# Linear attention and a gated feed-forward layer: the first batch's k and v on 128 partitions, and another order for the kernel's head

## The chip, the cores and the metric

The kernel runs on one core of a Trainium2 chip. Its engines work side by side, each through its own list of instructions in order: TensorE (PE in the profile, with its weight loads as PEld), VectorE (DVE), ScalarE (ACT), GpSimd (POOL) and SyncE (SP). They wait for one another by semaphores. DMA transfers are issued from the lists of SP, ACT and POOL. The metric is the device time of one execution in microseconds (us), the median of the runs.

## The reference

```python
batch, n_heads, seq, head_dim = (8, 8, 576, 64)

def _attn_ref(q, k, v, g_norm):
    kv = np.einsum('bhsd,bhse->bhde', k, v)
    out = np.einsum('bhsd,bhde->bhse', q, kv)
    rms = np.sqrt(np.mean(out * out, axis=-1, keepdims=True) + 1e-06)
    return (out / rms * g_norm).astype(np.float32)

def _moe_ref(x, w_gate, w_val, w_out):      # x: (4608, 512), d_ff 1536
    gate = 1.0 / (1.0 + np.exp(-(x @ w_gate)))
    val = x @ w_val
    return (gate * val @ w_out).astype(np.float32)
```

The attention has no softmax: for each head kv = k^T v (64 x 64, summed over the 576 tokens), then q times kv, then a norm over the 64 values. The heads of one token side by side are a row of x. q, k and v are float32, the three weights float64; the result is float32.

## The kernel before

The 4608 tokens are nine chunks of 512. Chunk 0 goes through a plain first and second layer (the last 64 tokens of batch 0 belong to chunk 1). Chunks 1 to 8 go through a version of the two layers that forms sums of blocks and needs fewer products (`first_layer_fast`, `second_layer_fast`, L1017 and L1120); its matmuls, L1037 and L1139, are most of the time. The change touches what comes before all this, called the head here: the attention of batch 0, the conversion of the first weight units, and the first two blocks of chunk 0's first layer.

**Loads.** `load_kv` (L91) and `load_q` (L100) load pair n (two heads) of batch 0, for n from 0 to 3, into the pool `first` with a buffer for each pair. Token s stands on partition s // 6, so a load of k or v has 96 partitions, and on each of them, for each of the two heads, six tokens in a row: 192 pieces of 1536 bytes. The loop at L298 issues on SP, in this order: k, v, q of pair 0; of pair 1; the gate half of weight unit 0; pair 2; the value half of unit 0; pair 3. Then `w1` and `w2` issue units 1 and 2 (`load_unit`, L153). A unit is a block of 128 columns of w_gate and of w_val, 512 KB each. It is staged as raw float64 in one of three buffers (`st`), so unit 3 can load only when unit 0 has been read, and so on.

**Conversion.** `convert` (L194) makes float32 weights of a staged unit: five steps on VectorE (s0 to s4) and two on ScalarE (a0 after s0, a1 after s1; s2 waits for a0, s3 for a1, s4 for s2 and s3). In the head, the two halves of units 0, 1 and 2 are converted one by one; s4 also multiplies by g_norm. From unit 3 on, `convert_step` does a unit at a time between the later matmuls.

**Attention of a pair** (`attention`, L335): KV is k^T v, `kv_mm` at L341, six steps j of 96 tokens and in each a matmul for either head, head e writing partitions 64e to 64e+63 of one PSUM bank; KVO copies it out on VectorE; Q turns q by six transposes (L356) and QO copies it on ScalarE; U multiplies, 20 matmuls of 64 x 64 (L373); SQ (ScalarE), SUM (VectorE), ROOT (ScalarE) and NORM (VectorE, reciprocal and product) are the norm; X transposes back (L400) and XO copies x to its place on ScalarE. One PSUM tile serves all Q, another bank all KV, and two tiles take U and X in turn: Q1 waits for QO0, KV1 for KVO0, U2 for XO0.

**Blocks.** `b0` and `b1` are the first two 128-column blocks of chunk 0's first layer (`Plain`, L659). `bf.i.m` is one matmul of 512 columns (L666): half i (gate or value) of block f with pair m of x. It needs that half's s4 and XO of pair m. G and E are the sigmoid and the product behind a block. `b0` uses the two banks that the fillers and KV use before.

**Order.** The pools are under a manual schedule: each engine gets its instructions in the order in which the program emits them. For the head this is the string `order` (L699), read token by token at L708: `KV0` or `XO3` is a step of a pair, `g1.3` or `v1.3` is step s3 of unit 1's gate or value half, `ag` and `av` are the ScalarE steps, `w3` loads unit 3, and `warm10` is ten matmuls of the identity with itself (L727), whose result nobody reads. Behind the head the dense stage runs: the other ten blocks of chunk 0 (`plain`, L678), with the attention of batch 1 between them, then its second layer.

Of the kernel before, what the change touches and what calls it, by code (L numbers as in the profile page):

```python
# [10 lines left out]
FP32 = mybir.dt.float32  # L11
# [10 lines left out]
def kernel(  # L22
# [11 lines left out]
    nc = tc.nc  # L34

    B, H, S, HD = q.shape
    T, DM = out.shape
    DF = moe_w_gate.shape[1]
    P = 128
    NHP = H // 2  # L40
    NJ = 6
    NP = S // NJ
    JH = NJ // 2


    PH = P // 2
# [38 lines left out]
    first = first_ctx.__enter__()  # L85
# [3 lines left out]
    pairs = {n: {} for n in range(B * NHP)}  # L89

    def load_kv(n):  # L91
        if n >= NE:
            return
        b, h0 = n // NHP, 2 * (n % NHP)
        for name, src in (("k", k), ("v", v)):
            t = first.tile([NP, 2, NJ * HD], FP32, tag=name, name=name)
            nc.sync.dma_start(out=t, in_=src[b, h0:h0 + 2].rearrange("h (p j) d -> p h (j d)", j=NJ))
            pairs[n][name] = t

    def load_q(n):  # L100
# [52 lines left out]
    def load_unit(u, halves=(0, 1)):  # L153
        if u >= len(units):
            return
        kind, f = units[u]
        if 0 in halves:
            staged[u] = raw.tile([P, 2, DM], I64, tag="st", name="st", bufs=NST)
        st = staged[u]
        for i in halves:  # L160
            if kind == "gv":
                src = (moe_w_gate, moe_w_val)[i].rearrange("(m p) f -> p m f", p=P)[:, :, P * f:P * f + P]
                nc.sync.dma_start(out=st[:, i].rearrange("p (m f) -> p m f", m=NMT), in_=src)
            else:
                nc.sync.dma_start(out=st[:, i], in_=moe_w_out[P * (f + i):P * (f + i) + P, :])
# [143 lines left out]
    w1 = const.tile([P, N3, 4 * NMT, 2, P], FP32, name="w1")  # L309
    w2 = const.tile([P, NFT, DM], FP32, name="w2")  # L310
    ident = const.tile([P, P], FP32, name="ident")
# [23 lines left out]
    def attention(n, at_ps):  # L335

        b, m = divmod(n, NHP)
        d = {}
        kv = kvq[:, m // 2, m % 2]

        def kv_mm():  # L341
            d["kv"] = ps = at_ps("kv")
            for j in range(NJ):
                js = slice(HD * j, HD * j + HD)
                for e in range(2):
                    nc.tensor.matmul(ps[HD * e:HD * e + HD, 0, 0:HD], pairs[n]["k"][:, e, js], pairs[n]["v"][:, e, js],  # L346
                                     start=(j == 0), stop=(j == NJ - 1))

        def kv_out():
            nc.vector.tensor_copy(out=kv, in_=d["kv"][:, 0, 0:HD])  # L350

        def q_mm():
            d["q"] = ps = at_ps("q")
            for j in range(NJ):
                c0 = NP * (j % JH)
                nc.tensor.transpose(ps[:, j // JH, c0:c0 + NP], pairs[n]["q"][:, j].rearrange("p e d -> p (e d)"),  # L356
                                    ident[0:NP, 0:NP])

        def q_out():
            d["qT"] = qTs[:, S * (n % 2):S * (n % 2) + S]  # L360
            nc.scalar.copy(out=d["qT"].rearrange("p (i n) -> p i n", i=2), in_=d["q"][:, :, 0:JH * NP])  # L361

        def u_mm():


            ps = at_ps("u")
            d["u"] = ps[:, :, 0:NU * HD]
            for i in range(2 * NU):
                t0 = min(PH * i, S - PH)
                r = PH * (i % 2)  # L370
                for e in range(2):
                    es = slice(HD * e, HD * e + HD)
                    nc.tensor.matmul(d["u"][r:r + PH, e, HD * (i // 2):HD * (i // 2) + HD],  # L373
                                     d["qT"][es, t0:t0 + PH], kv[es], start=True, stop=True)

        def u_square():
            d["sq"] = sqs[:, NU * P * (n % 2):NU * P * (n % 2 + 1)].rearrange("p (e c) -> p e c", e=2)
            nc.scalar.activation(out=d["sq"], in_=d["u"], func=AF.Square)

        def u_sum():  # L380
            d["ms"] = sb.tile([P, 2, NU], FP32, tag="ms", name="ms")
            nc.vector.tensor_reduce(out=d["ms"].rearrange("p e i -> p (e i)"),
                                    in_=d["sq"].rearrange("p e (i d) -> p (e i) d", d=HD), axis=AX.X, op=ALU.add)

        def u_root():
            nc.scalar.activation(out=d["ms"], in_=d["ms"], func=AF.Sqrt, bias=eps, scale=1.0 / HD)

        def u_norm():

            nc.vector.reciprocal(d["ms"], d["ms"])  # L390
            d["xn"] = d["sq"].rearrange("p e c -> p (e c)")
            nc.vector.tensor_tensor(out=d["xn"].rearrange("p (i e d) -> p e i d", e=2, d=HD),
                                    in0=d["u"].rearrange("p e (i d) -> p e i d", d=HD),
                                    in1=d["ms"].unsqueeze(3).to_broadcast([P, 2, NU, HD]), op=ALU.mult)

        def x_mm():
            d["x"] = ps = at_ps("x")
            for i in range(NU):
                bank, c0 = divmod(P * i, UX)
                nc.tensor.transpose(ps[:, bank, c0:c0 + P], d["xn"][:, P * i:P * i + P], ident)  # L400

        def x_out():

            s0 = 0
            while s0 < S:
                c, o = divmod(S * b + s0, G)
                i, r = divmod(s0, UX)
                n_ = min(G - o, (UX if i == 0 else S - UX) - r)
                nc.scalar.copy(out=chunk(c)[:, m, o:o + n_], in_=d["x"][:, i, r:r + n_])
                s0 += n_  # L410

        return [kv_mm, kv_out, q_mm, q_out, u_mm, u_square, u_sum, u_root, u_norm, x_mm, x_out]


# [220 lines left out]
    def at_ps():  # L635
        return psum.tile([P, NAT, 512], FP32, tag="at", name="at")
# [11 lines left out]
    warm, pair_kv = bank(0), bank(1)  # L648
# [29 lines left out]
    def plain(c, u, ps, steps_at):  # L678
# [18 lines left out]


    order = """  # L699
        w1 w2 warm10 KV0 warm4 Q0 KVO0 QO0 warm3 U0 KV1 KVO1 Q1 SQ0 QO1 SUM0 ROOT0 g0.0 warm4 U1 NORM0 SQ1 warm5 X0  # L700
        SUM1 ag0.0 ROOT1 g0.1 ag0.1 NORM1 XO0 warm1 KV2 Q2 KVO2 QO2 X1 g0.2 XO1 g0.3 warm2 U2 g0.4 v0.0 SQ2 b0.0.0
        v0.1 av0.1 SUM2 v0.3 b0.0.1 KV3 ROOT2 av0.0 NORM2 Q3 KVO3 X2 v0.2 w3 g1.0 QO3 U3 XO2 ag1.0 g1.1 ag1.1 SQ3 v0.4
        g1.2 v1.1 g1.3 v1.0 b0.0.2 av1.1 g1.4 v1.3 av1.0 b0.1.0 v1.2 w4 SUM3 b0.1.1 b0.1.2 v1.4 ROOT3 NORM3 g2.1 g2.0
        b1.0.0 b1.0.1 v2.1 ag2.1 b1.0.2 b1.1.0 X3 ag2.0 b1.1.1 XO3 g2.3 av2.1 b1.1.2 v2.0 b0.0.3 b0.1.3 av2.0 G0 g2.2
        g2.4 b1.1.3 v2.3 v2.2 v2.4 E0 b1.0.3 G1
    """
    blks = {}
    for token in order.split():  # L708
        name = token.rstrip("0123456789.")
        n = [int(i) for i in token[len(name):].split(".")]  # L710
        f = n[0]
        if name == "b":
            if f not in blks:
                if f:
                    two = early(NE)("q")
                blks[f] = Plain(0, F_ORDER[f], (two[:, 0], two[:, 1]) if f else (warm, pair_kv))
            blks[f].mm(n[1], n[2])
        elif name in ("G", "E"):
            (blks[f].gate if name == "G" else blks[f].end)()
        elif name in ("g", "v", "ag", "av"):  # L720
            m0 = NMT * (name[-1] == "v")
            conversion[f]["a" if name[0] == "a" else "c"][n[1]](slice(m0, m0 + NMT))
        elif name == "w":
            load_unit(f)
        elif name in ("warm", "warmk"):
            for _ in range(f):
                nc.tensor.matmul((warm if name == "warm" else pair_kv)[:, 0:P], ident, ident, start=True, stop=True)  # L727
        else:
            a[f][steps[name]]()
            if token == f"Q{NE - 1}":  # L730
                first_ctx.__exit__(None, None, None)
                hp = ctx.enter_context(tc.tile_pool(name="hp", bufs=1))
                h_main = [hp.tile([P, 4 * NT, P], FP32, name=f"h{j}") for j in range(N3)]
                h_more = hp.tile([P, N3, 3 * NT, P], FP32, name="h_more")
# [159 lines left out]
    for some in places.split():  # L894
        p, names = some.split(":")
# [6 lines left out]
    for f in range(2, NFT):  # L902
        if f == NFT - 1:
            last = at_ps()
            ps = last[:, 0], last[:, 1]
        else:
            ps = mm_ps(), mm_ps()
        plain(0, f, ps, {at: at_place.get(2 * NMT * (f - 1) + at, ()) for at in range(2 * NMT)})

    ps = [mm_ps() for _ in range(G // P)]  # L910
# [297 lines left out]
    X1 = (18, 19, 20, 21, 22, 22, 23, 23, 24, 24, 25, 26, 28, 30, 31, 33, 35, 37)  # L1208
    X2 = (14, 15, 16, 17, 19, 21, 24, 25, 25, 25, 25, 25, 25, 25, 25, 25, 25, 25)
    X3 = (7, 8, 11, 11, 12, 13, 14, 14, 16, 16, 19, 22, 22, 22, 22, 22, 23, 23)  # L1210
# [57 lines left out]
```

## Time and profile before

| | |
|---|---|
| Median of 3 runs | 996.44 us (996.24 to 997.7) |
| The profiled execution, its own time | 996.52 us |
| Its span, from the first to the last instruction | 994.7 us |
| Granted TensorE clock | 1.00 |
| DMA | 194.97 MB, mean 196 GB/s |

Busy time in the first 40 us, in us of each 10:

| From, to | PE | PEld | DVE | ACT | POOL | DMA share, GB/s |
|---|---|---|---|---|---|---|
| 0 to 10 | 8.60 | 8.16 | 0.43 | 2.26 | 0.70 | 0.82, 230 |
| 10 to 20 | 9.99 | 8.24 | 8.24 | 7.03 | 0.00 | 1.13, 295 |
| 20 to 30 | 9.95 | 5.35 | 9.69 | 5.87 | 6.32 | 1.05, 300 |
| 30 to 40 | 10.00 | 4.56 | 9.79 | 7.87 | 4.78 | 1.05, 253 |

In the rows of the profile L12 is line 12 of the kernel, `out<-in` are tiles by name, and xN counts records. A float32 matmul is two records, each with its own weight load; a transpose is one. A line of the chain of waits or of the timeline begins with its start and its length in us. "granted clock" tells only of the throttle: the speed at which matmuls really went is read from the distance between their records. TensorE's busy time is made of modelled ends, so a busy TensorE can still be a slow one. The DMA share can pass 1, since packets of one engine overlap.

### The profile page before, as it was taken

How to read it: one execution, taken by the hardware profiler on the slowest of the kernel's cores; microseconds unless marked ns; L12 is line 12 of the kernel's file. 1: busy time of each engine (PE TensorE's matmuls, PEld its weight loads, DVE VectorE, ACT ScalarE, POOL GpSimd, SP SyncE). 2: the span in 40 equal slices, each digit the busy share in tenths (PEclk: the TensorE clock that was granted, in tenths of full speed). 3: DMA queues.
4: the chain of work that ended last, by engine and by line, in shares of the span. 5: the costliest groups of instructions: out<-in, count | busy, mean ns of one | idle time of the engine just before them, and what ended most of it. 6: DMA issues, size and time to landing. Idle time of an engine off the chain costs nothing.

```text
span 994.7 us, 16605 instructions
## 1 busy us (share of the span) xinstructions
PE 989.4 (99%) x5958; PEld 814.9 (82%) x5958; DVE 715.0 (72%) x1199; ACT 349.1 (35%) x631; POOL 614.1 (62%) x991
## 2 busy tenths in 40 slices
PE   9999999999999999999999999999999999999998
PEld 7454448888888888888888888888888888888887
DVE  5999997898768666785777576866686566756672
ACT  5577523661244213530344124412442133213320
POOL 1349996798169625864386717870786359734963
PEclk9999999999999999999999999999999999999999
DMA  9986507662889568746975677656854455545514
GB/s 275 291 239 219 166 28 210 193 236 89 277 278 282 170 190 275 197 151 195 271 225 162 204 224 248 184 163 210 280 165 156 139 198 190 165 141 172 214 48 123
DMA packets 149523, 194.97 MB, mean 196 GB/s; under 512 B 79840, under 2 KB 121696, under 8 KB 149440
## 3 DMA queue, kind: packets, MB, share of 16 engines
q0 software_dynamic: 22512, 116.41, 35.3%
q1 hardware_dynamic: 120848, 75.66, 26.5%
q10 hardware_dynamic: 6080, 1.84, 0.8%
q8 instruction: 47, 0.77, 0.3%
q14 instruction: 36, 0.29, 0.1%
HBM read 160.04 MB, written 25.56 MB: 187 GB/s over the span
## 4 chain that ended last, share of the span: by engine, by line
PE 99%; ACT 0%; POOL 0%; issue 0%; DVE 0%; POOLq 0%; ACTq 0%
PE mm L1037 54%; PE mm L1139 27%; PE mm L666 7%; PE mm L913 4%; PE at L497 2%; PE mm L727 1%; PE at L447 1%; PE two L666 1%; PE at L666 1%; PE mm L447 1%; PE mm L346 0%; PE two L373 0%; PE two L356 0%; PE at L436 0%; PE two L400 0%; ACT qTs L361 0%
## 5 line engine op out<-in xcount | busy, mean ns | idle before, releaser
L1037 PE MATMUL mm<-xs,w 128*128 128x256 f32 x1428 | 331.3, 379 | 0.0
L1037 PEld LDWEIGHTS mm<-xs,w 128*128 128x128 f32 x1428 | 270.9, 190 | 37.0
L1037 PE MATMUL mm<-xT,w 128*128 128x256 f32 x948 | 230.5, 380 | 0.0
L1037 PEld LDWEIGHTS mm<-xT,w 128*128 128x128 f32 x948 | 179.6, 190 | 25.0 <-issue 0.5
L855 POOL DMA_DIRECT2D w<-kept x84 | 46.9, 559 | 203.1 <-PE mm L1037 199.6
L1007 DVE TENSOR_TENSOR sg<-sg,mm 128x512 f32<-128x512 f32 (+1 forms) x176 | 100.8, 600 | 89.8 <-PE mm L1037 34.3
L1139 PE MATMUL mm<-w,h 128*128 128x256 f32 x630 | 142.9, 379 | 0.0
L1139 PEld LDWEIGHTS mm<-w,h 128*128 128x128 f32 x630 | 119.6, 190 | 16.4 <-POOL h L999 0.2
L1003 ACT COPY temps<-mm 128x512 f32<-128x512 f32 (+1 forms) x128 | 66.0, 537 | 187.1 <-PE mm L1139 94.7
L999 POOL TENSOR_TENSOR h<-h,sg 128x512 f32<-128x512 f32 x72 | 96.6, 1360 | 46.0 <-ACT sg L996 30.2
L808 POOL TENSOR_TENSOR h<-h 128x128 f32<-128x128 f32 x216 | 110.5, 524 | 16.5 <-DVE h_more L808 13.1
L1139 PE MATMUL mm<-w,h_more 128*128 128x256 f32 x474 | 108.2, 379 | 0.0
L996 ACT ACTIVATE sg<-sg 128x512 f32<-128x512 f32 x96 | 59.7, 630 | 127.3 <-DVE sg L1007 127.3
L1139 PEld LDWEIGHTS mm<-w,h_more 128*128 128x128 f32 x474 | 90.1, 190 | 12.2
L1003 ACT COPY sg<-mm 128x512 f32<-128x512 f32 (+1 forms) x112 | 57.1, 510 | 87.5 <-PE mm L1139 45.3
L808 POOL TENSOR_TENSOR h_more<-h 128x128 f32<-128x128 f32 x120 | 58.6, 492 | 34.6 <-DVE h L999 30.3
L1007 DVE TENSOR_TENSOR temps<-temps,mm 128x512 f32<-128x512 f32 (+1 forms) x96 | 59.5, 620 | 26.6 <-PE mm L1139 16.9
L1007 DVE TENSOR_TENSOR temps<-mm,temps 128x512 f32<-128x512 f32 (+1 forms) x64 | 39.9, 623 | 53.3 <-PE mm L1139 23.9
L1003 ACT COPY h<-mm 128x512 f32<-128x512 f32 x48 | 28.1, 585 | 129.9 <-PE mm L1037 116.4
L666 PE MATMUL mm<-xT,w 128*128 128x512 f32 x160 | 70.1, 595 | 0.0
L1007 DVE TENSOR_TENSOR sg<-mm,sg 128x512 f32<-128x512 f32 (+1 forms) x64 | 39.7, 620 | 41.8 <-PE mm L1139 21.9
L808 POOL TENSOR_TENSOR h<-h,h_more 128x128 f32<-128x128 f32 x120 | 60.9, 508 | 4.6
(164 smaller groups left out, 1273.9 us busy)
## 6 DMA issues: line engine op xcount, KB each, us to landing
w<-kept POOLq DMA_DIRECT2D x42, 896.0 KB, 5.4
w<-kept POOLq DMA_DIRECT2D x90, 384.0 KB, 4.3
w<-kept POOLq DMA_DIRECT2D x42, 768.0 KB, 5.0
out_dram<-sg SPq DMA_DIRECT2D x119, 64.0 KB, 1.7
q<-in_q_dram SPq DMA_DIRECT2D x96, 72.0 KB, 5.0
xT<-xTs SPq DMA_DIRECT2D x96, 72.0 KB, 4.4
st<-in_moe_w_gate_dram SPq DMA_DIRECT2D x12, 512.0 KB, 6.2
st<-in_moe_w_val_dram SPq DMA_DIRECT2D x12, 512.0 KB, 6.4
```

Source lines behind the costliest of these rows:

```text
L447: nc.tensor.matmul(ps[m][HD * g:HD * g + HD, e], mains[2 * m + g, "k"][:, c], mains[2 * m + g, "v"][:, c], start=(b == 2 and e == 0 and j ...
L497: nc.tensor.matmul(to[HD * e:HD * e + HD], qTs[HD * g:HD * g + HD, c:c + HD], kvq[HD * g:HD * g + HD, m, e], start=True, stop=True)
L666: nc.tensor.matmul(self.ps[i], w[("wg", "wv")[i], self.f][:, m, :], xT[self.c][:, m, :], start=(m == 0), stop=(m == NMT - 1), skip_group_c ...
L808: ops.append((eng, lambda v=v, x=x, sign=sign, y=y, eng=eng: eng.tensor_tensor(out=h_form(v, j), in0=h_form(x, j), in1=h_form(y, j), op=op ...
L855: nc.gpsimd.dma_start(out=granule(g)[:, 0:n], in_=kept1[g // NPA % N3, g % NPA][:, 0:n])
L913: nc.tensor.matmul(ps[t], gv[0, f][:, P * t:P * t + P], w["wo", f], start=(f == 0), stop=(f == NFT - 1), skip_group_check=True)
L996: nc.scalar.activation(out=o["o" + step[1]], in_=o["o" + step[1]], func=AF.Sigmoid)
L999: mult.tensor_tensor(out=o[x], in0=o[x], in1=o[y], op=ALU.mult)
L1003: nc.scalar.copy(out=o[out_], in_=o[expr])
L1007: tt(out=o[out_], in0=o[x], in1=o[y], op=ALU.add if sign == "+" else ALU.subtract)
L1037: nc.tensor.matmul(regions[name][1][:, g], ws[:, g], xf[c][wv], start=(new and g == 0), stop=True, skip_group_check=True)
L1139: nc.tensor.matmul(regions[name][1], h_form(hv, j), ws[:, j], start=(used[i] and j == 0), stop=(j == N3 - 1), skip_group_check=True)
```

## The change

Pair n of batch 0 is laid out anew. Token s of head e now stands on partition 64e + s // 9, nine tokens in a row, so that the two heads share the 128 partitions and a load is 128 pieces of 2304 bytes. The tile has 640 columns, of which 576 are used. KV becomes nine steps j of 64 tokens, and a matmul of head e reads the partitions 64e to 64e+63 and writes the same partitions of the PSUM bank as before: 18 matmuls a pair in place of 12. Loads of q, and everything from batch 1 on, stay as they are.

A new token, `tiny`, issues matmuls without use that read a 64 x 64 corner of the identity and 16 columns of it. The order of the head is another: 15 `warm` matmuls in place of 29, and 54 `tiny`; KV, Q, U, X, the block matmuls, the conversion steps and `w3`, `w4` stand in other places, on TensorE's list and so on those of VectorE, ScalarE and SP.

```diff
+    JK = 2 * S // P
+    KVW = 640
...
         for name, src in (("k", k), ("v", v)):
-            t = first.tile([NP, 2, NJ * HD], FP32, tag=name, name=name)
-            nc.sync.dma_start(out=t, in_=src[b, h0:h0 + 2].rearrange("h (p j) d -> p h (j d)", j=NJ))
+            t = first.tile([P, KVW], FP32, tag=name, name=name)[:, 0:JK * HD]
+            nc.sync.dma_start(out=t, in_=src[b, h0:h0 + 2].rearrange("h (p j) d -> (h p) (j d)", j=JK))
             pairs[n][name] = t
...
             d["kv"] = ps = at_ps("kv")
-            for j in range(NJ):
+            for j in range(JK):
                 js = slice(HD * j, HD * j + HD)
                 for e in range(2):
-                    nc.tensor.matmul(ps[HD * e:HD * e + HD, 0, 0:HD], pairs[n]["k"][:, e, js], pairs[n]["v"][:, e, js],
-                                     start=(j == 0), stop=(j == NJ - 1))
+                    es = slice(PH * e, PH * e + PH)
+                    nc.tensor.matmul(ps[HD * e:HD * e + HD, 0, 0:HD], pairs[n]["k"][es, js], pairs[n]["v"][es, js],
+                                     start=(j == 0), stop=(j == JK - 1))
...
     order = """
-        w1 w2 warm10 KV0 warm4 Q0 KVO0 QO0 warm3 U0 KV1 KVO1 Q1 SQ0 QO1 SUM0 ROOT0 g0.0 warm4 U1 NORM0 SQ1 warm5 X0
-        SUM1 ag0.0 ROOT1 g0.1 ag0.1 NORM1 XO0 warm1 KV2 Q2 KVO2 QO2 X1 g0.2 XO1 g0.3 warm2 U2 g0.4 v0.0 SQ2 b0.0.0
-        v0.1 av0.1 SUM2 v0.3 b0.0.1 KV3 ROOT2 av0.0 NORM2 Q3 KVO3 X2 v0.2 w3 g1.0 QO3 U3 XO2 ag1.0 g1.1 ag1.1 SQ3 v0.4
-        g1.2 v1.1 g1.3 v1.0 b0.0.2 av1.1 g1.4 v1.3 av1.0 b0.1.0 v1.2 w4 SUM3 b0.1.1 b0.1.2 v1.4 ROOT3 NORM3 g2.1 g2.0
-        b1.0.0 b1.0.1 v2.1 ag2.1 b1.0.2 b1.1.0 X3 ag2.0 b1.1.1 XO3 g2.3 av2.1 b1.1.2 v2.0 b0.0.3 b0.1.3 av2.0 G0 g2.2
-        g2.4 b1.1.3 v2.3 v2.2 v2.4 E0 b1.0.3 G1
+        w1 w2 warm7 KV0 KVO0 warm1 Q0 QO0 warm6 U0 Q1 SQ0 SUM0 QO1 warm1 KV1 ROOT0 g0.0 KVO1 g0.1 tiny14 U1 NORM0
+        ag0.1 SQ1 g0.3 SUM1 KV2 ag0.0 g0.2 ROOT1 KVO2 tiny8 X0 Q2 XO0 NORM1 QO2 v0.1 v0.0 tiny24 U2 X1 g0.4 av0.1 SQ2
+        v0.3 tiny4 KV3 av0.0 SUM2 XO1 KVO3 ROOT2 Q3 v0.2 w3 NORM2 tiny4 b0.0.0 QO3 v0.4 g1.1 g1.0 U3 b0.0.1 SQ3 SUM3
+        ag1.1 ROOT3 X2 b0.1.0 XO2 b0.1.1 g1.3 v1.0 NORM3 ag1.0 av1.0 b0.0.2 g1.2 X3 XO3 b0.1.2 g1.4 v2.0 b1.0.0 v1.1
+        v2.1 g2.0 av2.0 av1.1 b1.0.1 v1.2 v1.3 w4 av2.1 ag2.0 g2.1 v2.3 b0.0.3 b0.1.3 v1.4 b1.0.2 ag2.1 g2.2 g2.3 v2.2
+        b1.1.0 G0 E0 b1.1.1 b1.1.2 g2.4 v2.4 b1.1.3 b1.0.3 G1
...
         elif name == "w":
             load_unit(f)
+        elif name == "tiny":
+            for _ in range(f):
+                nc.tensor.matmul(warm[0:PH, 0:PH // 4], ident[0:PH, 0:PH], ident[0:PH, 0:PH // 4], start=True, stop=True)
```

## The prediction

> **What bounds the kernel now.** I read the profile from the whole to the place of the change: busy time by engine, the chain of waits, that chain over the first 37 us, the timeline of TensorE around one group of small matmuls, and the landing times of the loads. First the page: engines, then shares of the chain that ended last.
>
> ```profile
> PE 989.4 (99%) x5958; PEld 814.9 (82%) x5958; DVE 715.0 (72%) x1199; ACT 349.1 (35%) x631; POOL 614.1 (62%) x991
> ...
> PE 99%; ACT 0%; POOL 0%; issue 0%; DVE 0%; POOLq 0%; ACTq 0%
> ```
>
> TensorE is the chain. The chain in order of time (start, length, what) shows where the change sits. A float32 matmul is two records, so x20 is warm10.
>
> ```profile
> 1.37 4.46 PE mm L727 x20
> 5.82 0.85 PE mm L346 x24
> 6.67 1.09 PE mm L727 x8
> ...
> 8.26 0.70 PE mm L727 x6
> ...
> 11.29 0.92 PE mm L727 x8
> 12.21 0.74 PE two L373 x40
> 12.95 1.31 PE mm L727 x10
> 14.26 0.55 PE two L400 x5
> 14.81 0.22 PE mm L727 x2
> 15.03 0.85 PE mm L346 x24
> ...
> 17.07 0.45 PE mm L727 x4
> ...
> 21.84 0.65 ACT qTs L361
> 22.50 0.04 issue
> 22.54 0.81 PE two L373 x40
> 23.35 3.63 PE mm L666 x8
> ...
> 34.74 1.72 PE two L666 x4
> 36.46 18.88 PE mm L666 x44
> ```
>
> From 1.37 on TensorE always has something, useful or not (L727 is the work of no use). At 36.46 the dense stage begins: 44 records of 512 columns in 18.88 us, 0.429 each, with no wait. The same holds to the end of the matmuls near 991. So a microsecond of TensorE time more or less before 36.46 moves the end by a microsecond, if the other engines follow. VectorE is the one to watch: from 30 to 40 us it is busy for 9.79 of 10.
>
> ```profile
> 30.00:40.00 10.00, 10.00 (x28) 4.56 (x27) 9.79 (x17) 7.87 (x12) 4.78 (x7) 1.00 1.05 253
> ```
>
> **The change part by part**, as TensorE time before the dense stage, against 36.46.
>
> *The start.* warm7 takes the place of warm10. At 0.223 a record (4.46/20) it ends at 1.37 + 14 x 0.223 = 4.49. KV0 needs v of pair 0, issued at 1.18 and landing 3.6 later: 4.8. KV0 starts near 4.86 where it was 5.82: -0.96.
>
> *k^T v.* Before, 12 matmuls are 24 records in 0.85 us. The two heads write different column halves and run two at a time: 12 steps of 0.058, and 0.15 to begin. Now there are 18 matmuls, 36 records, again two heads in different halves of columns, and of rows too: 18 x 0.058 + 0.15 = 1.20. Four times +0.35 is +1.40. The records of L727 go from 0.22 to 0.11 us each among the last of warm10, near 5.4, so some 0.54 us of KV0 runs at half speed, +0.27. Bounds: no row has fewer than 0.058 a step, so it isn't less; at most each of the 36 records takes a step of its own (a rival below). I take +1.67.
>
> *Fewer large fillers.* After KV0 the six groups of L727 took 1.09 + 0.70 + 0.92 + 1.31 + 0.22 + 0.45 = 4.69. Now warm1, warm6 and warm1 remain: 16 records of 0.111, and some 0.06 to begin each, 1.95. That is -2.74.
>
> *54 tiny matmuls* (14 + 8 + 24 + 4 + 4), 108 records with a 64 x 64 stationary operand and 16 columns to stream. No row has this form. Streaming alone gives a lower bound: 0.429/512 is 0.84 ns a column, 0.013 us a record, 1.45 us in all. The other bound is the 64-column weight load that each record brings. The four-way group U0 in the first 0.11 us:
>
> ```profile
> 8.98 0.21 PEld L373 LDWEIGHTS two<-kvq,qTs 64*64 64x64 f32 x8 [0.22 <-ACT qTs L361]
> 8.99 0.29 PE L373 MATMUL two<-kvq,qTs 64*64 64x64 f32 x4
> ```
>
> Eight weight loads have begun (two steps of four) but only four matmuls. A window that ends at 9.03 holds four loads and one that ends at 9.04 five, so the second step of loads comes 0.055 after the first with no matmul to wait for; the next matmuls start when those loads are through. Over whole groups the step is (0.67 - 0.134)/9 = 0.06 for U0 and (0.78 - 0.137)/11 = 0.058 for KV0. With 128 columns (8 records of L727 in 0.97) it is (0.97 - 0.19)/7 = 0.111. The step follows the columns of the stationary operand, and shrinking what is streamed to 16 doesn't shrink the load. The tinies all use the same quarter of the array, so they can't run side by side. I take 0.058: 108 x 0.058 = +6.26. If load and stream did not overlap, 0.071 a record, it would be 7.7. The Trainium skill ("TensorE: Matmul & The Clock Gate", "LDWEIGHTS (loading the stationary operand)") gives columns over 1.2 in ns, 53 ns here; the 0.055 agrees. The same page ("Wait — 56ns, not 53.3ns?") has starts of small matmuls down to 25 ns apart, which would make the tinies 2.7 us; that is a rival below.
>
> *Changes of shape.* KV and U show about 0.15 beyond their steps. The new KV, U and tinies share one 64 x 64 shape, so where they stand side by side (KV1-tiny-U1-KV2-tiny, tiny-U2, tiny-KV3) some of it goes; the tinies bring new changes beside Q, X and b. Between -0.8 (six saved at 0.15) and +0.4, I take -0.3.
>
> *Order and waits.* Q, U, X and the 32 records of the first two blocks stay as many. By order Q0 and Q1 now stand before their q has landed (6.9 and 9.9): some 0.5 us idle. Gone is the wait for QO3 at 21.76 to 22.54, of which X2 filled 0.55. Net +0.3; between 0 and +0.8.
>
> *What I cost at nothing.* The eight loads of k and v move the same bytes as 128 rows of 2304 B in place of 192 of 1536 B. Whatever they gain lies under TensorE's full queue from Q1 on; uncovered it would be worth what a load comes earlier. VectorE and ScalarE run the same instructions in another order, and with more filler TensorE is the later one: the last conversion of unit 2 ended at 35.97, 0.5 before the dense stage, and in the new order two block matmuls (1.7 us) stand behind it. If TensorE were not late, that 0.5 is all the cover there is. On SP, w3 waits for unit 0's staging buffer as before; w4 stands behind more VectorE work and goes out perhaps 4 us later than its 28.00. It landed at 37.1 and VectorE first needs it at 42.05, which moves later too; cover gone, unit 4 would be late by the rest, and the loads of unit 5 and batch 1 queue behind it on SP. POOL's queue of q loads gets its release with the last pair, as before. The narrower first pool only moves addresses.
>
> **Sum:** -0.96 + 1.67 - 2.74 + 6.26 - 0.3 + 0.3 = +4.2 us; the dense stage starts near 40.7. The profiled execution took 996.52 (span 994.7 and 1.8 around it; the median of the three runs is 996.44), so the forecast is **1000.7**. With the small terms at both ends it is 999.6 to 1001.8.
>
> **The rivals.**
>
> *A. The forecast,* 0.60: the tinies go at the pace of weight loads.
>
> *B. The tinies cost little,* and the last pair's landing decides. The second half of q3 is issued at 14.04:
>
> ```profile
> q<-in_q_dram SPq DMA_DIRECT2D x1, 144.0 KB, 6.6
> ```
>
> so it lands at 20.6. Behind it stand Q3 0.62, tiny4 0.2, b0.0.0 0.95 and U3 0.75, to 23.2; then 15 block matmuls of 0.858 (12.9), X2 and X3 (1.2) and 0.15 for changes: 37.4, +0.9, so **997.4**. Before, 14 block matmuls and one X were left when U3 ended at 23.35; now it is 15 and two. For it speaks the lower bound by streaming; against it the 0.055 above. The skill's floor of 25 ns would lead here; no row of this trace shows it. 0.18.
>
> *C. The two heads take turns.* In U and in the tails of batch 1 (L436) halves of rows that run side by side write different PSUM banks; in the new KV both write one bank. If that makes them take turns, 36 steps: 4 x 18 x 0.058 = 4.2 more, **1004.9**. No row has this case; other partitions are written, which speaks against it. The Trainium skill ("TensorEngine Tiling (Array Packing)", "Gotcha 1: PSUM Pressure") says that different row tiles cannot access the same bank simultaneously; by it the sum would be this one. 0.08.
>
> *D. The clock falls back.* The first 4 us ran at half speed. If thin work (tiny24, 16 columns) or the wait before KV0 brings one such stretch of 4 us, 2.0 more: **1002.7**. Against it, transposes and small groups from 14 to 18 us ran at full speed before. 0.07.
>
> *E. Not slower: earlier data pulls the head.* a load of 295 KB at the 0.31 MB per us moved around 10 us takes 0.95; at the 414 to 430 GB/s that the weight loads reach in single slices late in the trace, 0.7. Eight times 0.25 is 2.0: q3 lands at 18.6 and B's chain ends at 35.4, **995.5**. It decides only if the tinies are nearly free as well, and q3 must land over 0.9 us earlier to beat 36.46. Against it: with weights alone the queues move 0.34 MB per us, beside 0.31 with k and v in the mix. 0.07.
>
> **How the numbers follow.** The forecast is A's. The range 996.7 to 1002.8 holds A, B and D, 0.85, and leaves out C and E. About 0.2% (2 us) is what a measurement of this kernel can tell from no change. Slower by more: A, C and D, 0.75. Within it: B and E's larger part, 0.18 + 0.03. Faster by more: the far end of E, 0.04.
>
> **What would show it.** The group of the tinies: 108 records, a step of 0.058 (A) or under 0.03 (B). KV groups of 36 records in 1.2 us (2.25 is C). The dense stage near 40.7. Records of L727 or KV at double length after 6 us are D. k and v landing over 0.1 us earlier each is E's first half. I am wrong if TensorE waits between the tinies and U for more than a few tenths, or if the dense stage shows waits for VectorE.

## The result, and the profile after

| | before | after |
|---|---|---|
| Median, side by side on one chip | 996.93 us (996.24 to 997.7, 4 runs) | 1009.69 us (1007.44 to 1012.88, 4 runs) |
| Ratio | | 1.013, 95% interval 1.0095 to 1.0165 |
| The profiled execution, its span | 996.52, 994.7 | 1012.88, 1011.1 |
| Dense stage begins in it | 36.46 | 52.88 |
| Dense stage to the end of the span | 958.24 | 958.22 |

The kernel became slower by 1.3%, and the forecast of 1000.7 with its range up to 1002.8 lies below every run. The direction was right. The profiled execution of after is the slowest of its four, so its losses are at the upper end. The last two rows of the table say where to look: from the dense stage on, the two executions are equally long, so all of the 16.4 us arose in the head.

First the page of after: TensorE's busy time, and the clock in 40 slices of 25 us.

```profile
PE 1003.8 (99%) x6086; PEld 828.3 (82%) x6086; DVE 715.1 (71%) x1199; ACT 348.8 (34%) x631; POOL 613.0 (61%) x991
...
PEclk8799999999999999999999999999999999999999
```

TensorE is still busy for 99%, with 128 more matmul records, and 14.4 us more of "busy" time. Most of that is not more work: at half clock the same matmul counts as busy for about twice as long (below, 0.109 against 0.057 us a record). The 8 and the 7 at the left of PEclk are the sign; before, both are 9. The same in stretches of 10 us (busy time of each engine with its count, then the granted clock, the DMA share and GB/s):

```profile
10.00:20.00 10.00, 8.05 (x162) 7.75 (x161) 6.50 (x15) 3.36 (x7) 0.00 (x0) 0.79 1.05 302
20.00:30.00 10.00, 10.00 (x111) 9.33 (x109) 2.10 (x3) 3.74 (x9) 0.00 (x0) 0.50 0.38 129
30.00:40.00 10.00, 10.00 (x102) 6.86 (x102) 4.66 (x10) 2.70 (x7) 6.18 (x9) 0.52 0.53 157
```

The stretch from 40 to 50 us has 1.00 again. From 20 to 30 us TensorE runs at half clock without a gap, VectorE does 2.10 us of work where it did 9.69, and the DMA share falls from 1.05 to 0.38: everything waits for TensorE. The trace's clock records put the half clock from 15.75 to 39.64, which is 23.89 us or seven steps of 3.413. The chain of waits (start, length, what; L349 is KV, L376 U, L730 the tinies, L733 the large fillers, L669 the blocks):

```profile
1.37 3.36 PE mm L733 x14
...
4.80 1.57 PE mm L349 x36
...
10.29 1.20 PE mm L349 x36
11.48 1.53 PE mm L730 x27
13.01 0.68 PE two L376 x33
13.70 1.95 issue
15.64 0.31 PE two L376 x2
...
21.76 5.12 PE mm L730 x47
...
30.25 2.11 PE mm L349 x36
...
34.47 2.00 PE mm L669 x2
...
52.88 18.88 PE mm L669 x44
```

The first 27 tinies take 1.53 us, 0.057 each, as forecast. The next 47 take 5.12, 0.109 each; KV goes from 1.20 to 2.11, and a block matmul (two records) takes 2.00, where the forecast had 0.86. And there is a second thing that the forecast lacks: at 13.70 TensorE stops for 1.95 us in the middle of U1, and "issue" names nobody that it waits for. The list of TensorE's waits (total, times, longest) has it as one single wait, the longest of the execution:

```profile
PE two L376 <- issue: 1.9, 1, 1.9
```

### The profile page after: what moved, and what is told of

It is laid out like the page before. It is cut to its first block, busy times and chain, and to the rows that moved or that the text cites. A ratio compares the mean times of both kernels' runs of the same rounds, so it can differ in the third digit from the quotient of the medians.

```text
span 1011.1 us, 16854 instructions
## 1 busy us (share of the span) xinstructions
PE 1003.8 (99%) x6086; PEld 828.3 (82%) x6086; DVE 715.1 (71%) x1199; ACT 348.8 (34%) x631; POOL 613.0 (61%) x991
## 4 chain that ended last, share of the span: by engine, by line
PE 99%; issue 0%; POOL 0%; DVE 0%; POOLq 0%
PE mm L1043 54%; PE mm L1145 27%; PE mm L669 7%; PE mm L919 4%; PE at L500 2%; PE mm L730 1%; PE at L450 1%; PE mm L349 1%; PE at L669 1%; PE two L669 1%; PE mm L450 1%; PE mm L733 1%; PE two L376 0%; PE two L403 0%; PE two L359 0%; PE at L439 0%
## 5 line engine op out<-in xcount | busy, mean ns | idle before, releaser
L1043 PE MATMUL mm<-xs,w 128*128 128x256 f32 x1428 | 331.2, 379 | 0.0
L1043 PEld LDWEIGHTS mm<-xs,w 128*128 128x128 f32 x1428 | 270.9, 190 | 37.0
L1043 PE MATMUL mm<-xT,w 128*128 128x256 f32 x948 | 230.5, 380 | 0.0
L1043 PEld LDWEIGHTS mm<-xT,w 128*128 128x128 f32 x948 | 179.6, 190 | 25.0 <-issue 0.5
L814 POOL TENSOR_TENSOR h<-h 128x128 f32<-128x128 f32 x216 | 111.1, 527 | 16.6 <-DVE h_more L814 13.1
L669 PE MATMUL mm<-xT,w 128*128 128x512 f32 x160 | 72.3, 607 | 0.0
```

The costliest lines, as they stand in the source:

```text
L669: nc.tensor.matmul(self.ps[i], w[("wg", "wv")[i], self.f][:, m, :], xT[self.c][:, m, :], start=(m == 0), stop=(m == NMT - 1), skip_group_c ...
L814: ops.append((eng, lambda v=v, x=x, sign=sign, y=y, eng=eng: eng.tensor_tensor(out=h_form(v, j), in0=h_form(x, j), in1=h_form(y, j), op=op ...
L1043: nc.tensor.matmul(regions[name][1][:, g], ws[:, g], xf[c][wv], start=(new and g == 0), stop=True, skip_group_check=True)
```

## The experiments

Two questions are asked of the first eight kernels: which part of the change costs what, and whether the clock falls because TensorE stood still (the 1.95 us) or because the tinies are thin work. "Head" is the start of the dense stage in the profiled execution; "half again" the stretch at half clock after the clock had first been full; "wait" the longest stop of more than 0.15 us in the head that the profile puts down to nobody. Where the clock is said to be whole, the trace shows it for the profiled execution alone; of the other runs the record has the mean clock.

| Kernel | median us (runs) | before, beside it | ratio (95%) | head | half again | wait |
|---|---|---|---|---|---|---|
| before | | | | 36.46 | none | none |
| after | 1009.69 (1007.44 to 1012.88, 4) | 996.93 | 1.013 (1.0095 to 1.0165) | 52.88 | 23.89 | 1.95 |
| no_tiny | 1001.94 (1001.51 to 1002.96, 4) | 997.23 | 1.0053 (1.0036 to 1.007) | 37.79 | none | 0.96 |
| warm_for_tiny | 1001.28 (1000.86 to 1001.36, 4) | 997.23 | 1.0042 (1.0027 to 1.0057) | 41.04 | none | 0.22 |
| before_tiny | 1003.66 (1001.52 to 1004.74, 4) | 997.23 | 1.0064 (1.0049 to 1.0079) | 42.60 | 10.24 | 1.75 |
| before_new_kv | 998.27 (996.88 to 999.68, 10) | 997.23 | 1.0011 (1.0002 to 1.002) | 36.85 | none | none |
| first_warm | 1006.96 (1005.45 to 1011.91, 3) | 996.66 | 1.0115 (1.0072 to 1.0157) | 51.87 | 17.07 | 1.26 |
| tiny_moved | 1006.49 (1005.22 to 1014.51, 3) | 996.66 | 1.0121 (1.0058 to 1.0184) | 46.48 | 10.24 | 0.21 |
| long_warm | 1001.76 (1000.41 to 1006.78, 4) | 996.66 | 1.006 (1.003 to 1.009) | 42.41 | none | 0.46 |
| wide_tiny | 1001.63 (1000.71 to 1002.61, 3) | 996.66 | 1.005 (1.003 to 1.007) | 42.59 | none | 1.54 |
| after_again | 1007.13 (1006.81 to 1007.52, 3) | 997.0 | 1.0099 (1.0079 to 1.0118) | 46.78 | 13.65 | none |
| aligned_new_order | 997.66 (995.87 to 1001.04, 9) | 997.0 | 1.0006 (0.9994 to 1.0017) | 37.27 | none | none |
| aligned_old_order | 997.72 (996.49 to 998.73, 9) | 997.0 | 1.0004 (0.9994 to 1.0014) | 36.72 | none | none |
| narrow_tiny | 1002.99 (998.96 to 1009.06, 9) | 997.0 | 1.0066 (1.0044 to 1.0087) | 44.09 | 6.83 | 1.30 |

### The parts

**no_tiny**: after, without the tinies.

```diff
-        w1 w2 warm7 KV0 ... KVO1 g0.1 tiny14 U1 ... KVO2 tiny8 X0 ... v0.0 tiny24 U2 ... v0.3 tiny4 KV3 ... NORM2 tiny4 b0.0.0
+        w1 w2 warm7 KV0 ... KVO1 g0.1 U1 ... KVO2 X0 ... v0.0 U2 ... v0.3 KV3 ... NORM2 b0.0.0
```

> The changed kernel without its 54 tiny matmuls; nothing stands in their place, the rest of the order and the new layout of k and v stay. Theory T (the thin filler is the cause: it takes 0.057 us a record at full clock, and the clock falls to half because so little is done in it): the clock stays whole, the dense stage starts near 37, 996.5 to 997.5 us. Rival L (the layout, KV on halves of the rows, is what lets the clock fall): it falls here too, 1005 us or more. Rival S (the empty 1.95 us at 13.7, in which TensorE waits for nothing that the profile shows, is the cause, and comes from running through too many instructions too early): the gap is gone and the clock stays whole, as in T. If instead TensorE's own waits, now unfilled, are enough to let the clock fall, 1000 or more.

The clock stays whole, as theory T had it, and the dense stage begins at 37.79. The stop at 13.70 is gone, but one of 0.96 has come in U3, and the median is 1001.94 in place of 996.5 to 997.5: here span less head is 961.9, 3.7 more than in any other kernel. TensorE stops twice late in the span, each time for nobody, at the small matmuls of a later batch's attention (L450, L500):

```profile
496.28 1.14 PE at L500 x66
...
498.12 1.47 issue
...
710.48 1.14 PE at L500 x66
...
711.68 1.68 issue
```

The two stops are 3.15 of the 3.7. Count all of TensorE's instructions in the trace, its semaphore instructions with them. Then the stops that nobody ends stand behind the 449th (after; the expectations call this place the 450th row) and behind the 705th (the one of 0.96), the 6593rd and the 9409th (no_tiny): exactly a multiple of 256 apart. The page of after has a queue that carries instructions:

```profile
q8 instruction: 48, 0.79, 0.3%
```

48 packets in 0.79 MB, 16.4 KB each; TensorE has 12,436 instructions in after, or 259 a packet (before: 47 packets for 12,184). This suggests that the code arrives in pieces of 256 instructions, and that a burst of short matmuls can be through one piece before the next is there. The 54 tinies and the 24 more matmuls of KV, less 14 fillers, are 64 matmuls, or 256 instructions; with 4 semaphore instructions fewer, after has 252 more than before, all but one whole piece, so that every later boundary stands almost where it stood. no_tiny is 36 instructions off. That this is why it stops late is tried below.

**warm_for_tiny**: each group of tinies becomes half as many large fillers, about as long.

```diff
-        ... tiny14 U1 ... tiny8 X0 ... tiny24 U2 ... tiny4 KV3 ... tiny4 b0.0.0
+        ... warm7 U1 ... warm4 X0 ... warm12 U2 ... warm2 KV3 ... warm2 b0.0.0
```

> The changed kernel with every run of tiny matmuls replaced by half as many large fillers (7, 4, 12, 2 and 2 matmuls of 128 x 128 by 128 columns), which take the same time at full clock: 54 x 2 x 0.057 = 6.2 us against 27 x 2 x 0.111 = 6.0. Theory T: the clock stays whole, the dense stage starts at 40 to 41, 1000 to 1001 us, what the prediction's sum gave. Rival L: the clock falls all the same, 1006 us or more. Rival S: half as many instructions, so no gap and a whole clock, 1000 to 1001, as in T.

The same order, the same new KV, 54 records of 0.111 in place of 108 of 0.058, and the clock whole from 5.17 on:

```profile
18.36 2.71 PE mm L733 x24
...
41.04 18.88 PE mm L669 x44
```

The head ends at 41.04, against 40.7 forecast, and the median of 1001.28 is just above the 1000 to 1001 expected. So the order and the time that fillers take cost about what the sum says. What after loses beyond that comes with the kind of work that the tinies are.

**before_tiny**: before with its old KV and order, in which the 19 large fillers behind KV0 become 38 tinies.

```diff
-        w1 w2 warm10 KV0 warm4 Q0 KVO0 QO0 warm3 U0 ... warm4 U1 NORM0 SQ1 warm5 X0 ... warm1 KV2 ... warm2 U2
+        w1 w2 warm10 KV0 tiny8 Q0 KVO0 QO0 tiny6 U0 ... tiny8 U1 NORM0 SQ1 tiny10 X0 ... tiny2 KV2 ... tiny4 U2
```

> The kernel before, its order and its layout, with the 19 large fillers behind KV0 replaced by 38 tiny ones of the same time (0.22 us for each two). Theory T: the clock falls to half somewhere after 9 us and comes back when block matmuls fill a stretch; 5 to 16 us slower than before. Rival L: the old layout keeps the clock, within 1 us of before. Rival S: whether a gap shows decides; without one, within 1 us of before.

The old kernel, with the same TensorE time by the sum, falls to half clock for 10.24 us, and behind instruction 449 it stops for 1.75. It is 6.4 us slower, within theory T's 5 to 16. Neither the order nor the layout is needed for the loss.

**before_new_kv**: before with the new loads and the new KV alone (the diff's first three parts).

> The kernel before with the new layout of k and v alone (128 partitions, 18 matmuls a pair), its order and large fillers kept. Theory T: no loss of clock; four times 0.35 us more of TensorE work, which partly takes the place of nothing else, so 1.0 to 1.5 us slower, 997.5 to 998.5. Rival L: the clock falls, 1003 or more. If the loads landing earlier were worth anything it would show here as less than 1.0.

The new layout costs +0.11% (0.02 to 0.2) by itself, as theory T expected. Its KV groups take 1.20, or 1.05 beside a group of the same shape, against 0.85. Two heads do write one PSUM bank side by side; taking turns would be 2.25. The last half of q3 lands at 18.83 in place of 20.62, yet TensorE can't use it: Q3 ends at 22.50, where before it ended at 21.77.

### Standing still, or thin work

**first_warm**: `tiny14`, in front of the stop, becomes `warm7`; the other 40 tinies stay.

> The changed kernel with only its first run of tinies, tiny14 before U1, replaced by warm7; tiny8, tiny24 and both tiny4 stay. Theory S, as the first four runs shaped it (TensorE comes to its 450th row before the next 16 KB of its code are there, stands empty for 1.75 to 1.95 us, and the clock falls at the end of the 3.4 us stretch that holds this): TensorE reaches that row after 15 us, as with large fillers everywhere, the gap is under 0.5 us, the clock stays whole and the time is 1000.5 to 1002. Theory T (thin filler alone lets the clock fall): it falls in or behind tiny24, 1004 or more.

TensorE stops again for 1.26 us behind instruction 449, now in KV2 instead of U1, where theory S expected less than 0.5. The clock is at half for 17.07 from 20.54 on: before tiny24, which starts at 21.72, and not in or behind it, as theory T expected. No tiny stands ahead of this stop, so the stop comes with the boundary and not with the tinies. Both possible causes of the fall are still there.

**tiny_moved**: the 14 tinies go from U1 to U2.

```diff
-        ... g0.1 tiny14 U1 ... v0.0 tiny24 U2
+        ... g0.1 U1 ... v0.0 tiny38 U2
```

> The changed kernel with all 54 tinies kept, but the 14 before U1 moved to the 24 before U2: 38 in one run, 4.3 us of thin work at full clock, longer than one stretch of the clock's control. Theory S: TensorE is later at its 450th row, the gap is under 0.5 us, the clock stays whole, 1000.5 to 1002. Theory T: the clock falls behind the 38, 1004 or more.

Here the stop is gone but for 0.21, and the clock still falls at 19.56, for 10.24 us, in the middle of the long group of tinies. The chain, and a stretch of 10 us:

```profile
17.20 6.13 PE mm L730 x75
```

```profile
20.00:30.00 10.00, 10.00 (x130) 9.22 (x130) 1.92 (x5) 2.16 (x6) 0.00 (x0) 0.51 0.37 129
```

So TensorE needn't stand still for the clock to fall: theory S had the stop right and the clock wrong.

**long_warm**: `tiny24`, the longest group, becomes `warm12`; the other 30 stay.

> The changed kernel with only tiny24 replaced by warm12; the tiny14 before U1 stays. Both theories: the gap of nearly 2 us at the 450th row is there, and the clock falls near 15.7. What differs is the way back: if the thin filler keeps the clock down (S starts the fall and T prolongs it), warm12 fills one stretch at half clock and the full clock is back near 26, as in the old order with tinies, 1004 to 1006; if the clock simply stays down a fixed time of 24 us, 1009 or more.

Both theories expected a stop of nearly 2 us and a fall near 15.7. The stop is 0.46 and the clock of the profiled execution stays whole. One of four runs took 1006.78, with a mean clock of 0.996 where the others have 0.999 or 1: with 30 tinies it falls sometimes.

**wide_tiny**: as many tinies, with the same 64 x 64 stationary operand, but each streams 64 columns in place of 16.

```diff
-                nc.tensor.matmul(warm[0:PH, 0:PH // 4], ident[0:PH, 0:PH], ident[0:PH, 0:PH // 4], start=True, stop=True)
+                nc.tensor.matmul(warm[0:PH, 0:PH], ident[0:PH, 0:PH], ident[0:PH, 0:PH], start=True, stop=True)
```

> The changed kernel with tinies that stream 64 columns in place of 16: as many instructions, and by the weight-load pace about as long (0.058 us a record). If thinness prolongs the slow stretch: the gap at the 450th row stays, the clock falls, but comes back after one to three stretches, 1003 to 1006. If the streamed columns set the pace of the tinies, they take four times as long and the dense stage is later still. If what counts is only that little of the array is used (64 x 64 of it), as before: 1008 to 1012.

This is the kernel that decides, and none of the three expected outcomes came: the clock does not fall at all. Its chain has the stop of 1.54 us at the same place:

```profile
12.27 1.57 PE mm L730 x27
...
14.48 1.54 issue
...
19.50 2.88 PE mm L730 x47
```

and its next stretch has the clock at 1.00 in place of 0.50:

```profile
20.00:30.00 10.00, 10.00 (x195) 8.16 (x194) 6.43 (x12) 5.08 (x11) 3.67 (x6) 1.00 0.57 191
```

The tinies take 0.058 to 0.061 a record, against 0.057 with 16 columns, so streaming four times as much is nearly free. The mean clock is 1.000 in all three runs. It was 0.988 to 0.993 in all seven runs of after (with after_again), and 0.988 to 0.996 in the six of first_warm and tiny_moved, measured beside wide_tiny on the same chip. A stop of 1.54 us didn't let the clock fall here; with streams of 16 columns it falls with the stop and, in tiny_moved, without it. Without the stop, wide_tiny's head would end at 42.59 - 1.54 = 41.05, next to warm_for_tiny's 41.04.

### A second trace of after, and the boundary

**after_again**: after, unchanged.

> The changed kernel unchanged, for a second trace of it. If what was read from its first trace is its usual course, TensorE waits 1 to 2 us for nothing that the profile shows before U2 (at row 450 of its matmuls), the granted clock is at a half for three to seven steps of 3.4 us (10 to 24 us), and the time is 1005 to 1013. If the half clock of the first trace was an accident of one execution, the time is 1000 to 1002 here.

The fall is no accident, but the stop isn't there in every execution. This chain goes through the same place, instruction 449 in U1, with no wait:

```profile
13.76 0.68 PE two L376 x35
14.44 1.05 PE mm L349 x36
...
17.58 3.03 PE mm L730 x47
```

and the next stretch is at half clock all the same:

```profile
20.00:30.00 10.00, 10.00 (x114) 7.81 (x112) 4.09 (x8) 2.81 (x7) 2.45 (x4) 0.50 0.48 163
```

The instruction packet in question starts at 11.61 here and at 13.11 in after; in after, wide_tiny (13.39) and narrow_tiny (12.82) TensorE goes on 2.5 to 2.6 us after that start. By that, an estimate, it is ready here at some 14.2, which is when TensorE reaches the place. The expected wait of 1 to 2 us was wrong, the half clock (13.65, from 20.07) and the time as expected. So without the stop this execution still took 1006.81 us.

**aligned_new_order** and **aligned_old_order**: new loads and KV with only five large fillers, which keeps the count of TensorE's instructions as before (12,180 and 12,184). The first has the new order without tinies, the second the order of before.

```diff
-        w1 w2 warm7 KV0 KVO0 warm1 Q0 QO0 warm6 U0 ... warm1 KV1 ... tiny14 U1 ... tiny8 X0 ... tiny24 U2 ... tiny4 KV3 ... tiny4 b0.0.0
+        w1 w2 warm4 KV0 KVO0 Q0 QO0 warm1 U0 ... KV1 ... U1 ... X0 ... U2 ... KV3 ... b0.0.0
```

> The new order and layout with 5 large fillers and no tiny ones, so that TensorE has as many instructions as in the kernel before. If the number of instructions decides where the later waits stand (theory: they come where a packet of 256 instructions begins in a bad place), the waits of 1.5 and 1.7 us near 498 and 712 us that the kernel without tinies showed are gone, and the time is 996.5 to 999. If the waits belong to the order and not to the count, they stay and the time is 1000 or more. With so few fillers the clock may rise late or fall again; then the start of the dense stage, not the later stages, shows it.

> The order of before and the new layout, with 5 large fillers in place of 29: again as many TensorE instructions as before. The start of the dense stage should come near 36 to 38 (36.85 with all the fillers), since the fillers that are gone stood where TensorE waits for data, and the rest of the span is as long as before: 996 to 998.5. If the fillers hold the clock, it rises later than 10 us or falls again, and the time is 999 or more.

The late stops are gone from the new order. Its matmuls of the fast layers (L1043) now run on behind the same two places, without a stop:

```profile
496.94 23.08 PE mm L1043 x106
...
709.40 10.77 PE mm L1043 x49
```

With ten large fillers less than no_tiny the median is 4.3 us lower, 997.66. Both expectations came true. So it is the count that placed those stops, and not the order. Not every other count does harm: warm_for_tiny (144 instructions off) and before_new_kv (96) have no late stop. Both aligned kernels equal before (1.0006 and 1.0004, both intervals hold 1); neither beats it. Their clocks first became full late, at 13.51 and 8.95, and their heads end at 37.27 and 36.72 all the same. One of the nine runs of the new order has a mean clock of 0.996 and took 1001.04.

**narrow_tiny**: after with a stationary operand of 32 columns, streaming 16 as before.

```diff
-                nc.tensor.matmul(warm[0:PH, 0:PH // 4], ident[0:PH, 0:PH], ident[0:PH, 0:PH // 4], start=True, stop=True)
+                nc.tensor.matmul(warm[0:PH // 2, 0:PH // 4], ident[0:PH, 0:PH // 2], ident[0:PH, 0:PH // 4], start=True, stop=True)
```

> The changed kernel with a stationary operand of 32 columns in the tiny matmuls in place of 64; they stream 16 columns as before. If the weight load sets their pace, a record takes about 0.03 us at the full clock in place of 0.057, and the 54 cost 3 us less. If it is the little that they stream that lets the clock fall, it falls here too: half clock for 10 us or more, and the time is 1000 or more (about 3 us, or at half clock up to 6, below the changed kernel of the same job). If the clock stays whole, the time is 997.5 to 999.

```profile
12.37 0.98 PE mm L730 x28
...
18.57 1.62 PE mm L730 x48
```

0.034 to 0.035 a record against 0.057: the pace goes with the columns of the stationary operand. The time is 4.1 us below after_again, as expected. In the profiled execution the clock is at half for 6.83, less than the 10 expected. It falls in six of nine runs. Their times go with it: 998.96, 1000.81 and 1001.19 at a mean clock of 1.000; 1002.48 to 1005.66 from 0.997 to 0.993; 1009.06 at 0.990.

## Why the prediction failed

**The terms of the sum held at full clock.** KV0 started at 4.80 (4.86 forecast), a KV group took 1.20 (1.20), a tiny record 0.057 (0.058). The streaming width made hardly a difference to that, the stationary width did, so the pace is that of the weight load, as read from U0. The Trainium skill ("TensorE: Matmul & The Clock Gate", "LDWEIGHTS (loading the stationary operand)") makes 53 and 27 ns of 64 and 32 columns; 57 and 34 were measured. The head of two kernels whose clock stayed whole ended at 41.04 and, less its stop, at 41.05: 4.6 in place of 4.2 by the sum. With that, 1000.7 would have been 1001.1; warm_for_tiny has 1001.28 and wide_tiny, with its stop, 1001.63. (The two terms with bounds, shape and order, give 999.9 to 1001.9 by their own numbers, where the text has 999.6 to 1001.8. Nothing hangs on it.)

**The failed step is rival D, the clock.** The sum took 0.058 for every tiny record and so put a fall of the clock at nothing. As a rival it was seen, but priced at one stretch of 4 us, 2.0 us, and given 0.07. In all seven runs of after the clock fell; in the two traces the half clock lasted 23.89 and 13.65 us. Taking 41.05 and the stop away, it cost 52.88 - 41.05 - 1.95 = 9.9 us and 46.78 - 41.05 = 5.7, some 0.42 us for each us at half clock. The 16.4 us of the profiled execution are then 4.6 of work, 1.95 of the stop and 9.9, the rest, of the clock. Two arguments led astray. "One stretch of 4 us" took the start of the kernel as the length of a fall; in the traces of the new order the clock came back 6.5 to 13.1 us behind the end of the tinies at U2, and the half clock itself puts that end off. And "transposes and small groups ran at full speed before" compared the tinies with groups such as KV and U, which stream 64 columns. That such groups hold the clock was right: they do in the aligned kernels with hardly a filler, in 17 of 18 runs. Sixteen columns are another matter, which no row of before showed.

**Order and waits, +0.3 with at most +0.8,** was short by a stop, by the counts a wait for code. It cost 1.95 in one execution of after and nothing in the other. The text named no such cause, but a wait of more than a few tenths between the tinies and U was among its signs of being wrong, and the stop came next to that place, in U1 behind tiny14.

**The other rivals.** B (cheap tinies) fell with 0.057 a record. C (two heads in one bank take turns) fell with 18 steps in 1.05 to 1.20; the rule quoted from the Trainium skill ("TensorEngine Tiling (Array Packing)", "Gotcha 1: PSUM Pressure") didn't hold here, for halves of rows that write different partitions of one bank. E was half right: q3 landed 0.9 us earlier in after and 1.8 in before_new_kv, and TensorE was too late to use it.

**Why the clock falls** was only named in general, as thin work. Shown is: with the number of records, their stationary operand and their pace unchanged, 16 streamed columns let it fall and 64 don't. The Trainium skill ("TensorE: Matmul & The Clock Gate", "What's actually happening") says that a monitor of activity sets the clock by free-running windows of 3413 ns. The trace agrees in that: all stretches at half clock in the table, 6.83 to 23.89 us, are multiples of 3.413. The Trainium skill, in the same section, has the clock go down after an idle window, and there the runs differ: in tiny_moved and after_again TensorE had no wait of over 0.1 us in the 3.4 us ahead of the fall.

The kept traces allow one count more. Cut the time at full clock into its steps of 3.413 us, and add up in each the columns streamed by the matmuls that start in it, each matmul weighted with its rows over 128. Of the 4001 steps of the 14 traces up to 990 us, the six that end in a fall have 1040 to 1536, and all the others 1728 or more. In after the step with the stop has 1360, in wide_tiny 1824; in after_again and tiny_moved, without the stop, the tinies alone bring it to 1040 and 1152. So the stop and thin work look like two ways to the same end. It also fits that before_tiny falls (1192) while aligned_old_order, with nothing in the fillers' places, doesn't (2864 at least): there more useful work falls into each step. The weight was chosen after the fact (columns alone don't separate the steps), and no kernel was made to test it. It doesn't explain the way back: at half clock steps with 1560 and 1600 led back to full, and three with 1984 didn't. So how activity is counted stays open.

## What to carry to other kernels

Work of no use that is meant to keep the clock up has to stream columns: with 64 stationary columns, 64 streamed cost hardly more than 16 (0.058 to 0.061 us a record against 0.057), and the thin filler cost the clock that it should hold. Before adding a filler, take it away: five did here what 29 did. When a small edit changes the number of an engine's instructions, look for stops without a cause far behind it, a multiple of 256 instructions apart, before blaming the edit's own place.

## What the runs showed of the hardware that was not expected

- The granted clock was 0.5 for three to seven steps of 3.413 us while TensorE was busy without a gap (tiny_moved: 9.22 us of weight loads in 10, at 0.51).
- TensorE's stops without a cause stand a multiple of 256 instructions apart, and its code comes in packets of 16.4 KB. Where TensorE had stopped, it went on 2.3 to 2.6 us after the packet's start, and the stop cost 0.2 to 2.0 us. What sets that start wasn't found.
- The moment of the first full clock differs between executions: 5.17 to 10.29 us in the nine traces whose order is the same up to KV1.
